# Joining 32x32 triangular inverses: four products beside each other, one transpose moved, and new due places, in a fused delta-rule attention and two feed-forward layers

## The chip, the cores and the metric

The kernel runs on one core of one Trainium2 chip (8 cores on the chip, 7 of them unused). The metric is the device time of one execution in microseconds (us). Before the change it is 960.64 us, the median of 3 runs (959.18 to 965.52 us).

## The reference, cut to what matters

Three layers in fp32: a delta-rule attention over 768 tokens (4 batches, 8 heads, head size 48), whose output of 3072 x 384 goes through a feed-forward layer with a squared ReLU (384 to 2048 to 384) and one with a maximum of three products (384 to 768 to 384).

```python
k_n = k / (np.linalg.norm(k, axis=-1, keepdims=True) + 1e-06)
for t in range(S):
    kt, vt, bt = (k_n[:, :, t], v[:, :, t], beta[:, :, t, None])
    y[:, :, t] = np.einsum('bhd,bhde->bhe', q[:, :, t], state)
    v_old = np.einsum('bhde,bhd->bhe', state, kt)
    state = state + bt[:, :, :, None] * np.einsum('bhd,bhe->bhde', kt, vt - v_old)
...
h = x @ w_in
r = np.maximum(h, 0.0)
out = (r * r) @ w_out
...
h = np.maximum(np.maximum(x @ w1, x @ w2), x @ w3)
out = h @ w_out2
```

## The kernel before, in words

**Stages.** The 768 tokens of each sequence are cut into six stages t of 128 tokens, and each stage into two chunks c of 64. A stage of attention is `gram(t)` (line 516: products of keys with keys into G, of queries with keys into W), `solve(t)` (line 602: the inverse of a triangular 64x64 matrix for each of 32 units, 16 for each chunk), `values(t)` and `chain(t)` (line 742: the state is carried through both chunks; the stages of it are Removed, Updates, State and `outputs`). `rows` (line 826) then sends the chunk's output from Y to xr with ten small transfers, `split` (line 861) splits xr into a high part xh and a low part xl, and `moe1(t)` (line 908) runs the first feed-forward layer for that stage: 16 slices f of w_in, each three matmuls of xh and xl with wih and wil for each of three rows of 128, then gh and gl with the slice of w_out, in fp32r. Where t is 0 the weights are prepared on the way (`load_w`, line 873: two passes on ScalarE, seven on VectorE for each of 32 pieces). For t = 0 the first 8 slices are done for the two chunks separately. The second feed-forward layer comes last, from about 540 us on. fp32 matmuls (attention) show as two instructions each in the trace, fp32r matmuls (the layers) as one.

**The inverse.** T is the inverse of each unit's triangular matrix of 64, in blocks of 32. Partitions hold four blocks of 32: two (0 to 31 and 32 to 63) for one head of a pair, two (64 to 95 and 96 to 127) for the other. A VectorE loop over 31 columns inverts all 32x32 diagonal blocks, two instructions a column (tmp, then T). T is transposed into Tn. The off-diagonal block is then made from two products with the block of K K^T that joins the halves: `solve` multiplies the joining block (in G, upper partitions, columns 32 to 63) with Tn into M1 (lines 697 to 711), and M1 with the transposed T in G into the result (lines 724 to 739). Both loops go over c, then n, then p0 in (0, 64); each matmul is 32x32, and the two of one n are on different partitions. ScalarE brings the sets of 64 matmuls from PSUM to M1 (four instructions of 32x512) and to G with a factor -1 (four of 32x512). Between the sets VectorE transposes T into columns 32 to 63 of G, ScalarE copies them to columns 0 to 31 on partitions 0 and 64, and POOL clears the lower left blocks. M1 is the memory of L.

```python
pl.vector.transpose(out=Tn.rearrange("p u k -> p k u"), in_=T.rearrange("p i k -> p k i"))
...
pl.vector.transpose(out=G[:, :, 32:64].rearrange("p u i -> p i u"), in_=T)
```

**What sets the order.** No engine's program is written by hand. Every call on `pl` is recorded (class `_Engine`, line 279; the call itself is made at line 324, which is therefore the line of all rows) with a cost and a due place `pl.at`, in units of one matmul group, 96 to a stage (TICKS). `Planner.issue` (line 253) plays the list forward from the due places, goes back from the end to get new due places, does so eight times, and issues the best order. Constants (line 375) set the due places: BOOST pulls an eviction ahead, DEC the weight pieces, CL the chain, GL the next `gram` and `solve`, SPL the reloads of w_out, LATE the second chunk in stage 0. MIX, FULL, STAY, BURST and URGENT (line 61) say when the planner goes from small fp32 matmuls to large fp32r ones and back. `together(beside=True)` makes several matmuls one step that is counted as lying beside each other; `gram` and `chain` use it, `solve` does not. The queues: all transfers are issued from SP. TensorE writes to eight PSUM banks: 0 to 2 for the results of `moe1`, 3 for its hidden part, 4 and 5 for `gram` and `solve`, 6 and 7 for `chain`; in stage 0 other rings are used, `first_ring` for the first chunk's chain (banks 2, 3, 0; line 840).

Of the kernel before, what the change touches and what calls it, by code (L numbers as in the profile page):

```python
# [52 lines left out]
class Planner:  # L53
# [6 lines left out]
    MIX, FULL, STAY, BURST, URGENT = 3816, 7024, 12.67, 1.78, 3.70  # L60
    INTO, BACK = 0.09, 0.2
    HOLD = {"vector": 0.06}
    LAG = {"tensor": 0.2, "vector": 0.13, "scalar": 0.15, "gpsimd": 0.08, "sync": 0.0}

    def __init__(self, nc):
        self.nc, self.at, self.ops, self.seen, self.joint, self.beside = nc, 0.0, [], {}, None, False
        self.free, self.first, self.end, self.before_all = {}, 0, {}, False
# [11 lines left out]
    def add(self, engine, call, cost, outs, ins, flow, late):  # L79
        if self.joint is None or self.joint == len(self.ops):  # L80
            self.ops.append([engine, [], 0.0, set(), self.at, any(a.dtype == F32R for a in ins), 0.0, 0.0, self.before_all])
# [32 lines left out]
    def forward(self, at):  # L114
# [20 lines left out]
        while todo:  # L135
# [14 lines left out]
            while r and r[0][0] <= t + self.HOLD.get(e, 0.0):  # L150
                when, n = heappop(r)
                heappush(q, (at[n], n))
                start[n] = when
# [24 lines left out]
            if e == "tensor":  # L178
# [4 lines left out]
                late = ops[n][7]  # L183
                if ticks.get(tick - 1, 0.0) < 3060:
                    cost *= 2
                    late *= 2
# [7 lines left out]
            if e == "sync":  # L194
                free[e] = t + 0.6
                free["dma"] = max(t + 1.3, free.get("dma", 0.0)) + cost
                end[n] = free["dma"] + 1.0
            else:
                free[e] = end[n] = t + cost
                if e == "tensor":  # L200
                    end[n] += late
# [77 lines left out]
class _Engine:  # L279
# [3 lines left out]
    def __getattr__(self, what):  # L283
        fn = getattr(getattr(self.plan.nc, self.name), what)

        def record(*args, **kw):
# [5 lines left out]
            cols = out.free_size()  # L292
# [13 lines left out]
            elif self.name == "vector":  # L306
                fast = what in ("tensor_scalar", "tensor_copy") and space != PSUM
                cost = (cols / (2 if fast else 1) + 64) / 960
                if what == "transpose":
                    cost = (cols * 1.8 + 64) / 960  # L310
                elif what == "reciprocal":
                    cost = (cols * 6 + 64) / 960
            elif self.name == "scalar":
# [7 lines left out]
            flow = late = 0.0  # L321
# [8 lines left out]
def kernel(  # L330
# [44 lines left out]
    GL, CL, G1, DEC, BOOST, SPL, CUT, HALF, G2, LATE, EARLY, BLOCKS, FIRST = 27, 51, -1, 97, 147, 41, 6, 8, -135, 155, 0, 3, 2  # L375
# [69 lines left out]
    Lx = one(apool, [P, 2, 528], F32, "L")  # L445
    Tx = one(apool, [P, 2, 528], F32, "T")
    L, T = (x.rearrange("p b n -> p (b n)")[:, 0:1024].rearrange("p (i k) -> p i k", i=32) for x in (Lx, Tx))
    Ld, Td = (x[:, :, 0:512].rearrange("p b (i k) -> p b i k", i=16)[:, :, :, 0:16] for x in (Lx, Tx))
    low = one(apool, [P, 2], F32, "low")
# [66 lines left out]
    def gram(t, at):  # L516

        pl.at = at
# [17 lines left out]
        def products(units, keys, queries):  # L536
# [65 lines left out]
    def solve(t, at):  # L602

        pl.at = at
# [26 lines left out]
        small = t < EARLY  # L631
        if small:
            for j in range(15):
                n, m = 15 - j, j + 1
                parts = (slice(0, 1), slice(1, 2)) if t == 0 else (slice(0, 2),)
                tv = [
                    tmp[:, 128 * x.start:128 * x.start + (x.stop - x.start) * n * m].rearrange(
                        "p (b n m) -> p b n m", n=n, m=m)
                    for x in parts
                ]  # L640
                for v, x in zip(tv, parts):
                    shape = [P, x.stop - x.start, n, m]
                    pl.vector.tensor_tensor(
                        v,
                        Ld[:, x, j + 1:16, j:j + 1].to_broadcast(shape),
                        Td[:, x, j:j + 1, 0:m].to_broadcast(shape),
                        op=ALU.mult,
                    )
                for v, x in zip(tv, parts):
                    pl.vector.tensor_tensor(  # L650
                        Td[:, x, j + 1:16, 0:m], Td[:, x, j + 1:16, 0:m], v, op=sub
                    )
                if j % 2:
                    adv(3)
        for j in range(0 if small else 31):
# [16 lines left out]
        if small:  # L672

            for c in range(2):
                px = a_ring().rearrange("p (u k) -> p u k", k=32)
                for u in range(NP):
                    for p0 in range(0, P, 32):
                        pl.tensor.matmul(
                            px[p0:p0 + 32, u], G[p0:p0 + 32, NP * c + u, 0:32],
                            Tn[p0:p0 + 32, NP * c + u], start=True, stop=True,  # L680
                        )
                pl.scalar.activation(M1[:, NP * c:NP * c + NP], px, AF.Copy)
            pl.vector.transpose(out=G[:, :, 0:32].rearrange("p u i -> p i u"), in_=T)
            for x in range(2):
                pz = a_ring().rearrange("p (u k) -> p u k", u=NU)
                for u in range(NU):
                    for p0 in range(0, P, 32):
                        p = slice(p0, p0 + 32)
                        left, right = (M1[p, u], G[p, u, 16:32]) if x else (G[p, u, 0:32], M1[p, u, 0:16])
                        pl.tensor.matmul(pz[p, u], left, right, start=True, stop=True)  # L690
                old = G[:, :, 16:32] if x else Tn[:, :, 0:16]
                pl.vector.scalar_tensor_tensor(
                    old, pz, low[:, x:x + 1], old, op0=ALU.mult, op1=ALU.add
                )
            adv(2)
        M1c, Gc = (x.rearrange("p (n c) k -> p c n k", c=2) for x in (M1, G))
        for c in range(2):
# [11 lines left out]
            for p0 in (32, 96):  # L709
                pl.scalar.activation(M1c[p0:p0 + 32, c], pm[p0:p0 + 32], AF.Copy)  # L710
            adv(1)
        pl.at -= LATE * (t == 0)
        if small:
            for p0 in (32, 96):
                pl.scalar.activation(G[p0:p0 + 32, :, 32:64], G[p0:p0 + 32, :, 0:32], AF.Copy)
                pl.gpsimd.memset(G[p0:p0 + 32, :, 0:32], 0.0)
        else:
            for p0 in (32, 96):
                pl.gpsimd.memset(G[p0:p0 + 32, :, 0:32], 0.0)
            pl.vector.transpose(out=G[:, :, 32:64].rearrange("p u i -> p i u"), in_=T)  # L720
            for p0 in (0, 64):
                pl.scalar.activation(G[p0:p0 + 32, :, 0:32], G[p0:p0 + 32, :, 32:64], AF.Copy)
        adv(2)
        for c in range(2):
            pl.at += LATE * c * (t == 0)
            pm = a_ring().rearrange("p (n x) -> p n x", n=NP)
            for n in range(NP):
                u = 2 * n + c
                for p0 in (0, 64):
                    pl.tensor.matmul(  # L730
                        pm[p0:p0 + 32, n, :],
                        M1[p0 + 32:p0 + 64, u, :],
                        G[p0 + 32:p0 + 64, u, 32:64],
                        start=True, stop=True,
                    )
            for p0 in (0, 64):
                pl.scalar.activation(
                    Gc[p0:p0 + 32, c, :, 32:64], pm[p0:p0 + 32], AF.Copy, scale=-1.0
                )
            adv(1)  # L740

    def chain(t, at):
        pl.at = at
# [82 lines left out]
        def rows(c):  # L826
            xv = xr.rearrange("p r (b c x) -> p r b c x", b=B, c=2)
            Yv = Y.rearrange("p (b a) x -> p a b x", b=B)
            for h in range(H):
                f0, e0 = h * D, 0  # L830
                while e0 < D:
# [3 lines left out]
                    pl.sync.dma_start(  # L835
                        out=xv[o:o + n, r, :, c, :], in_=Yv[p0:p0 + n, h // 2]
                    )
                    e0 += n

        first_ring = Ring([banks[2], banks[3], banks[0]])  # L840
# [145 lines left out]
    with tc.manual_schedule():  # L986
        make_identity(nc, ident)
        nc.gpsimd.memset(mask, 1.0)
        for p0 in (0, 64):
# [4 lines left out]
        nc.vector.tensor_reduce(  # L994
            out=low[:, 0:1], in_=ident.rearrange("p (q x) -> p q x", x=32)[:, :, 16:32],
            axis=mybir.AxisListType.XY, op=ALU.add, negate=True,
        )
        nc.vector.tensor_scalar(low[:, 1:2], low[:, 0:1], -1.0, -1.0, op0=ALU.mult, op1=ALU.add)
# [152 lines left out]
```

## Time and profile before

| | us |
|---|---|
| median of 3 runs | 960.64 |
| lowest and highest | 959.18, 965.52 |
| profiled execution | 961.32 |
| its span, first to last instruction | 959.4 |
| TensorE busy in the span | 889.5 (93%) |
| VectorE busy | 595.4 (62%) |
| ScalarE busy | 444.9 (46%) |
| mean granted clock of TensorE | 0.957 |

The rows name engines PE (TensorE matmuls), PEld (its weight loads), DVE (VectorE), ACT (ScalarE), POOL (GpSimd) and SP (the issuing of transfers). A row gives what is written, then what is read; a note in square brackets is the idle time of the engine just before and what ended it. Matmuls overlap, so their durations are longer than the distance between starts.

### The profile page before, as it was taken

Reading aid. Unit: us, or ns where it says so; the run is one execution under the profiler, and the core shown is the slowest. Engines: PE = TensorE matmul, PEld = TensorE weight load, DVE = VectorE, ACT = ScalarE, POOL = GpSimd, SP = SyncE. Lnnn points to the kernel's source line nnn. Section 1 sums busy time; section 2 is a strip of 40 time slices with the busy share of each in tenths; the row PEclk is TensorE's granted clock in tenths of the full one; section 3 lists DMA queues with packets and bytes.
Section 4 is the critical chain, followed back from the end, with each engine's and each line's share of the span. In section 5 each row is a group of like instructions: output and inputs, shape, how many; then the busy total and the mean of one; then the engine's idle time right before and its main releaser. Section 6 shows DMA issues by size and latency. Waiting matters only on the chain.

```text
span 959.4 us, 22394 instructions
## 1 busy us (share of the span) xinstructions
PE 889.5 (93%) x9388; PEld 745.0 (78%) x9388; DVE 595.4 (62%) x1258; ACT 444.9 (46%) x817; POOL 23.7 (2%) x33
## 2 busy tenths in 40 slices
PE   5446798999989998999999999999999999999998
PEld 4336698776877787877877788888898989898987
DVE  5999997899848966875963389893323232322221
ACT  6355367684365564475455567663222212121111
POOL 2001000010000000000000000000000000000000
PEclk9655799999999999999999999999999999999999
DMA  9754475677734745534522567661020100000000
GB/s 167 157 128 116 84 217 161 155 171 184 188 75 93 178 102 97 142 101 95 123 68 75 175 189 229 191 196 68 1 67 1 67 1 26 8 25 9 25 9 33
DMA packets 186276, 100.65 MB, mean 105 GB/s; under 512 B 150080, under 2 KB 166208, under 8 KB 186176
## 3 DMA queue, kind: packets, MB, share of 16 engines
q1 hardware_dynamic: 186176, 99.22, 40.1%
q8 instruction: 74, 1.21, 0.5%
q14 instruction: 26, 0.21, 0.1%
HBM read 79.53 MB, written 14.94 MB: 98 GB/s over the span
## 4 chain that ended last, share of the span: by engine, by line
PE 76%; DVE 13%; SPq 4%; DMA 3%; ACT 2%; issue 2%; DVEq 0%; ACTq 0%
PE ps L324 76%; SPq L324 4%; DVE xs L324 2%; DVE tmp L324 2%; DVE T L324 2%; DVE W L324 1%; DVE t L324 1%; DMA xr<-Y 1%; DMA qt<-in_q_dram 1%; ACT G L324 1%; DVE wo L324 1%; DVE gl L324 1%; DVE L L324 0%; DVE Tn L324 0%; DVE G L324 0%
## 5 line engine op out<-in xcount | busy, mean ns | idle before, releaser
L324 PE MATMUL ps<-gh,wo 128*128 128x512 f32 (+1 forms) x624 | 159.4, 385 | 3.3 <-ACT gh L324 1.7
L324 DVE TENSOR_TENSOR r<-r,ps 128x512 f32<-128x512 f32 x72 | 49.5, 688 | 178.7 <-PE ps L324 176.6
L324 ACT ACTIVATE r<-ps 128x512 f32<-128x512 f32 (+1 forms) x140 | 80.3, 573 | 157.0 <-PE ps L324 148.8
L324 PEld LDWEIGHTS ps<-gh,wo 128*128 128x128 f32 x624 | 112.2, 191 | 28.3 <-ACT gh L324 1.9
L324 PE MATMUL ps<-xh,wih 128*128 128x512 f32 (+1 forms) x312 | 123.4, 395 | 1.7 <-ACT r L324 1.7
L324 PE MATMUL ps<-xh,wil 128*128 128x512 f32 (+1 forms) x312 | 119.3, 382 | 0.3 <-DVE wil L324 0.3
L324 PE MATMUL ps<-xl,wih 128*128 128x512 f32 (+1 forms) x312 | 119.4, 383 | 0.0
L324 DVE TENSOR_TENSOR gl<-r,gh 128x512 fp32r<-128x512 f32 (+1 forms) x104 | 67.0, 645 | 40.6 <-ACT gh L324 37.3
L324 PE MATMUL ps<-gl,wo 128*128 128x512 f32 (+1 forms) x312 | 85.4, 382 | 0.0
L324 PEld LDWEIGHTS ps<-xh,wih 128*128 128x128 f32 x312 | 59.8, 192 | 15.5 <-ACT r L324 2.9
L324 PEld LDWEIGHTS ps<-xl,wih 128*128 128x128 f32 x312 | 59.9, 192 | 12.2
L324 PEld LDWEIGHTS ps<-xh,wil 128*128 128x128 f32 x312 | 60.1, 193 | 11.3 <-DVE wil L324 0.7
L324 ACT ACTIVATE gh<-r 128x512 fp32r<-128x512 f32 (+1 forms) x104 | 62.0, 596 | 10.9 <-PE ps L324 8.5
L324 PEld LDWEIGHTS ps<-gl,wo 128*128 128x128 f32 x312 | 56.4, 190 | 12.0
L324 DVE TENSOR_TENSOR tmp<-L,T 128x31 f32<-128x31 f32 (+15 forms) x186 | 62.9, 338 | 3.8
L324 DVE TENSOR_TENSOR T<-T,tmp 128x31 f32<-128x31 f32 (+15 forms) x186 | 62.9, 338 | 3.4
L324 ACT ACTIVATE r<-r 128x512 f32<-128x512 f32 (+1 forms) x104 | 62.1, 597 | 2.5
L324 PE MATMUL ps<-W 64*64 64x64 f32 x1536 | 44.8, 244 | 12.4 <-ACT W L324 11.3
L324 ACT ACTIVATE G<-ps 32x256 f32<-32x256 f32 (+2 forms) x96 | 46.4, 483 | 16.5 <-PE ps L324 14.7
L324 PEld LDWEIGHTS ps<-W 64*64 64x64 f32 x1536 | 37.7, 154 | 20.0 <-ACT W L324 14.0
L324 DVE TENSOR_SCALAR xs<-xs 128x384 f32<-128x384 f32 (+1 forms) x112 | 42.3, 380 | 16.4 <-ACT xs L324 15.5
L324 ACT ACTIVATE m0h<-r 128x512 fp32r<-128x512 f32 x18 | 11.4, 632 | 67.2 <-DVE r L324 67.2
(147 smaller groups left out, 1671.2 us busy)
## 6 DMA issues: line engine op xcount, KB each, us to landing
wo<-wod SPq DMA_DIRECT2D x88, 384.0 KB, 3.2
raw<-in_moe_w_out_dram SPq DMA_DIRECT2D x22, 384.0 KB, 3.6
raw<-in_moe_w_dram SPq DMA_DIRECT2D x18, 384.0 KB, 3.8
raw<-in_moe_w_in_dram SPq DMA_DIRECT2D x16, 384.0 KB, 4.1
wod<-wo SPq DMA_DIRECT2D x16, 384.0 KB, 3.2
vn<-in_v_dram SPq DMA_DIRECT2D x24, 192.0 KB, 4.5
kn<-in_k_dram SPq DMA_DIRECT2D x24, 192.0 KB, 4.9
out_dram<-ob SPq DMA_DIRECT2D x24, 192.0 KB, 1.9
```

The lines of the kernel that those rows point to most:

```text
L324: self.plan.add(self.name, lambda: fn(*args, **kw), cost, [out], ins, flow, late)
```

## The change

- In `solve`, the two products join the halves from the left in the even chunk (joining block times Tn, then the other half's inverse) and from the right in the odd one (the inverse in the upper partitions first, then Tn of the lower). A group of four matmuls, one step for the planner, lies on four blocks of partitions and four of results. The number of matmuls is the same, 64 a set.
- T is transposed straight into columns 0 to 31 of G, right behind the transpose into Tn and ahead of the first set; copies on partitions 32 and 96 bring it to columns 32 to 63, and the clearing on POOL follows the second set. One copy of 128x512 to M1 takes the place of four of 32x512.
- `gram` writes the lower joining block of the odd units as well, two more ScalarE copies for each call of `products` with odd units.
- In `rows`, five of the ten transfers of stage 0's first chunk are issued from ScalarE. `first_ring` has six places on four banks.
- The planner: MIX, BURST and HOLD change, the later ready time of large matmuls' results in the model is dropped, and nearly all due places change, with one offset for each stage of `gram`, `solve` and `chain`. EARLY was 0 and HURRY is 0: what hangs on them is not run.

```diff
-    MIX, FULL, STAY, BURST, URGENT = 3816, 7024, 12.67, 1.78, 3.70
-    INTO, BACK = 0.09, 0.2
-    HOLD = {"vector": 0.06}
+    MIX, FULL, STAY, BURST, URGENT = 3719.33, 7024.00, 12.67, 2.43, 3.70
+    INTO, BACK, RUSH = 0.09, 0.2, 0.52
+    HOLD = {"vector": 0.071}
...
-    GL, CL, G1, DEC, BOOST, SPL, CUT, HALF, G2, LATE, EARLY, BLOCKS, FIRST = 27, 51, -1, 97, 147, 41, 6, 8, -135, 155, 0, 3, 2
+    GL, CL, G1, DEC, BOOST, SPL, CUT, HALF, G2, LATE, BLOCKS, FIRST, HURRY = 27, 46, -1, 97, 164, 47, 6, 8, -133, 228, 3, 2, 0
+    GRAM = (0, -8, 0, 23, 17, 0)
+    SOLVE = (0, 0, 0, 80, 12, -33)
+    CHAIN = (-9, -8, 0, 11, -5, -19)
...
                     pl.scalar.activation(Gu[p, :, 0:32], pk[p, :, 32:64], AF.Copy)
+                    odd = slice(1, n, 2) if units.step is None else slice(0, n * (units.start % 2))
+                    if odd.stop:
+                        pl.scalar.activation(Gu[p, odd, 32:64], pk[p, odd, 0:32], AF.Copy)
...
-        for c in range(2):
-            pl.at += LATE * c * (t == 0)
-            pm = a_ring().rearrange("p (n x) -> p n x", n=NP)
-            for n in range(NP):
-                u = 2 * n + c
+        pl.vector.transpose(out=G[:, :, 0:32].rearrange("p u i -> p i u"), in_=T)
+
+
+        pm = a_ring().rearrange("p (n x) -> p n x", n=NP)
+        for n in range(NP):
+            with pl.together(beside=True):
                 for p0 in (0, 64):
+                    lo, hi = slice(p0, p0 + 32), slice(p0 + 32, p0 + 64)
+                    pl.tensor.matmul(pm[hi, n], G[lo, 2 * n, 32:64], Tn[lo, 2 * n], start=True, stop=True)
                     pl.tensor.matmul(
-                        pm[p0 + 32:p0 + 64, n, :],
-                        G[p0:p0 + 32, u, 32:64],
-                        Tn[p0:p0 + 32, u, :],
+                        pm[lo, n], G[hi, 2 * n + 1, 32:64], G[hi, 2 * n + 1, 0:32],
                         start=True, stop=True,
                     )
...
+        pl.scalar.activation(M1[:, 0:NP], pm, AF.Copy)
+        adv(1)
+        pa, pb = (a_ring().rearrange("p (n x) -> p n x", n=NP) for c in range(2))
+        for n in range(NP):
+            with pl.together(beside=True):
                 for p0 in (0, 64):
...
+                    lo, hi = slice(p0, p0 + 32), slice(p0 + 32, p0 + 64)
+                    pl.tensor.matmul(pa[lo, n], M1[hi, n], G[hi, 2 * n, 0:32], start=True, stop=True)
+                    pl.tensor.matmul(pb[lo, n], Tn[lo, 2 * n + 1], M1[lo, n], start=True, stop=True)
+        Gc = G.rearrange("p (n c) k -> p c n k", c=2)
+        for p0 in (0, 64):
+            for c, px in enumerate((pa, pb)):
+                p = slice(p0, p0 + 32)
+                pl.scalar.activation(Gc[p, c, :, 32:64], px[p], AF.Copy, scale=-1.0)
+        for p0 in (32, 96):
+            p = slice(p0, p0 + 32)
+            pl.scalar.activation(G[p, :, 32:64], G[p, :, 0:32], AF.Copy)
+            pl.gpsimd.memset(G[p, :, 0:32], 0.0)
...
-                    pl.sync.dma_start(
-                        out=xv[o:o + n, r, :, c, :], in_=Yv[p0:p0 + n, h // 2]
-                    )
+                    queue = pl.scalar if t + c == 0 and h % 2 else pl.sync
+                    queue.dma_start(out=xv[o:o + n, r, :, c, :], in_=Yv[p0:p0 + n, h // 2])
...
-        first_ring = Ring([banks[2], banks[3], banks[0]])
+        first_ring = Ring([banks[x] for x in (2, 3, 0, 7, 2, 3)])
```

## Rows read from the trace of the kernel before

**Rows 1.** The page: engines, slices of the span and a DMA queue (packets, MB, share).

```profile
PE 889.5 (93%) x9388; PEld 745.0 (78%) x9388; DVE 595.4 (62%) x1258; ACT 444.9 (46%) x817; POOL 23.7 (2%) x33
...
PE   5446798999989998999999999999999999999998
...
DVE  5999997899848966875963389893323232322221
...
PEclk9655799999999999999999999999999999999999
...
q8 instruction: 74, 1.21, 0.5%
```

**Rows 2.** Five stretches: busy us (instructions) of each engine, granted clock, DMA share, GB/s.

```profile
101.00:144.00 43.00, 40.03 (x547) 37.20 (x544) 41.19 (x108) 25.13 (x60) 0.00 (x0) 0.85 0.61 163
144.00:192.00 48.00, 43.12 (x927) 38.27 (x926) 37.40 (x79) 34.98 (x72) 1.27 (x2) 0.96 0.60 158
192.00:226.00 34.00, 31.08 (x217) 23.38 (x216) 32.77 (x82) 23.60 (x45) 4.06 (x6) 1.00 0.78 183
226.00:502.00 276.00, 268.35 (x4191) 217.18 (x4191) 206.26 (x420) 148.17 (x259) 8.62 (x9) 0.99 0.51 118
502.00:960.00 458.00, 453.25 (x2419) 383.61 (x2419) 189.53 (x344) 163.37 (x289) 0.00 (x0) 1.00 0.23 73
```

**Rows 3.** Timeline of PE: the a joining set of stage 1 and one of stage 2.

```profile
145.06 1.83 PE L324 MATMUL ps<-G,L 32*32 32x32 f32 x102
149.19 0.62 PE L324 MATMUL ps<-G,L 32*32 32x32 f32 x26 [2.31 <-issue]
...
265.82 2.21 PE L324 MATMUL ps<-Tn,G 32*32 32x32 f32 x128
267.96 0.50 PE L324 MATMUL ps<-xh,wih 128*128 128x512 f32 x1
```

**Rows 4.** Timeline of PE: a set of `gram`, four beside each other.

```profile
196.61 1.16 PE L324 MATMUL ps<-W 64*64 64x64 f32 x64
197.70 0.73 PE L324 MATMUL ps<-gh,wo 128*128 128x512 f32 x2
```

**Rows 5.** Timeline of all engines, 74 to 88 us: the tail of `solve(0)`.

```profile
74.34 1.92 DVE L324 STREAM_TRANSPOSE Tn<-T 128x1024 f32<-128x1024 f32 x1
...
76.31 3.63 PE L324 MATMUL ps<-Tn,G 32*32 32x32 f32 x128 [7.05 <-DVE Tn L324]
...
80.10 1.93 DVE L324 STREAM_TRANSPOSE G<-T 128x1024 f32<-128x1024 f32 x1
...
82.18 3.62 PE L324 MATMUL ps<-G,L 32*32 32x32 f32 x128 [2.24 <-DVE G L324]
...
85.73 2.54 PE L324 MATMUL ps<-vn,G 64*64 64x48 f32 x38
...
87.94 0.98 POOL L324 MEMSET G<- 32x1024 f32 x1 [4.83 <-DVE L L324]
```

**Rows 6.** Groups of ACT by shape: count, busy us, mean ns, idle before.

```profile
L324 ACT ACTIVATE G<-ps 32x256 f32<-32x256 f32 x48 | 18.1, 376 | 1.0
...
L324 ACT ACTIVATE L<-ps 32x512 f32<-32x512 f32 x24 | 14.2, 591 | 6.6 <-PE ps L324 6.4
...
L324 ACT ACTIVATE G<-G 32x1024 f32<-32x1024 f32 x12 | 12.7, 1054 | 1.8 <-DVE G L324 1.6
```

**Rows 7.** Timelines of SP and ACT: the first row transfers of stage 0.

```profile
95.60 7.31 SPq L324 DMA_DIRECT2D xr<-Y  x10
...
98.95 0.42 ACT L324 ACTIVATE xh<-xr 128x256 fp32r<-128x256 f32 x1 [3.37 <-DMA xr<-Y]
```

**Rows 8.** PE's waits, 226 to 960 us (us, times, longest), and a DMA queue (packets, MB, share), 265 to 300 us.

```profile
PE ps L324 <- issue: 4.9, 6, 2.3
...
q8 instruction: 8, 0.13, 1.5%
```

**Rows 9.** Groups of DVE: the column loop of `solve`.

```profile
L324 DVE TENSOR_TENSOR tmp<-L,T 128x31 f32<-128x31 f32 (+15 forms) x186 | 62.9, 338 | 3.8
```

More of the change, by code (lines that the diff above doesn't have):

```diff
@@ L66, in __init__ @@
         self.nc, self.at, self.ops, self.seen, self.joint, self.beside = nc, 0.0, [], {}, None, False
-        self.free, self.first, self.end, self.before_all = {}, 0, {}, False
+        self.free, self.first, self.end, self.before_all, self.rush = {}, 0, {}, False, False
         self.flow, self.ticks, self.start = (deque(), False, False), {}, {}
@@ L80, in add @@
         if self.joint is None or self.joint == len(self.ops):
-            self.ops.append([engine, [], 0.0, set(), self.at, any(a.dtype == F32R for a in ins), 0.0, 0.0, self.before_all])
+            self.ops.append([engine, [], 0.0, set(), self.at, any(a.dtype == F32R for a in ins), 0.0, 0.0, self.before_all, self.rush])
         n = len(self.ops) - 1
@@ L149, in forward @@
             r = ready.get(e, [])
-            while r and r[0][0] <= t + self.HOLD.get(e, 0.0):
+            hold, later = self.HOLD.get(e, 0.0), []
+            while r and r[0][0] <= t + (self.RUSH if hold else 0.0):
                 when, n = heappop(r)
-                heappush(q, (at[n], n))
-                start[n] = when
+                if when <= t + hold or ops[n][9]:
+                    heappush(q, (at[n], n))
+                    start[n] = when
+                else:
+                    later.append((when, n))
+            for x in later:
+                heappush(r, x)
             n = q[0][1]
@@ L199, in forward @@
                 free[e] = end[n] = t + cost
-                if e == "tensor":
-                    end[n] += late
+                if e == "scalar":
+                    end[n] += ops[n][7]
             todo -= 1
@@ L291, in record @@
                 ins.append(out)
-            cols = out.free_size()
+            cols, late = out.free_size(), 0.0
             space = ins[0].space if ins else None
@@ L312, in record @@
                     cost = (cols * 6 + 64) / 960
+            elif what == "dma_start" and self.name == "scalar":
+                cost, late = 0.65, 2.0
             elif self.name == "scalar":
@@ L320, in record @@
                 cost = words / row * 0.00142 if row < 128 else words * 4 / (220e3 if row < 512 else 290e3)
-            flow = late = 0.0
+            flow = 0.0
             if self.name == "tensor":
@@ L444 @@
     bl = one(apool, [P, NS, 32], F32, "bl")
[L445 to L449, printed above, removed]
+    L = one(apool, [P, 32, 32], F32, "L")
+    T = one(apool, [P, 32, 32], F32, "T")
     st = one(apool, [P, 5, 32], F32, "st")
@@ L516, in gram @@
     def gram(t, at):
-        pl.at = at
+        pl.at = at + GRAM[t]
         W, G = W2[t % 2], GG[t % 2]
@@ L630, in solve @@
         adv(2)
[L631 to L647, printed above, removed]
-                    )
[L649 to L655, printed above, removed]
+        for j in range(31):
             n, m = 31 - j, j + 1
@@ L671, in solve @@
         adv(2)
-        if small:
-            for c in range(2):
[L675 to L695, printed above, removed]
@@ L713, in solve @@
[L713 to L722, printed above, removed]
@@ L723, in solve @@
[L723 to L728, printed above, removed]
-                for p0 in (0, 64):
[L730 to L740, printed above, removed]
+        pl.scalar.activation(M1[:, 0:NP], pm, AF.Copy)
@@ L742, in chain @@
+        for p0 in (0, 64):
[6 more added lines that the diff above has]
+            pl.gpsimd.memset(G[p, :, 0:32], 0.0)
+        adv(1)
+        pl.rush = False
     def chain(t, at):
-        pl.at = at
+        pl.at = at + CHAIN[t]
@@ L993 @@
             )
[L994 to L998, printed above, removed]
         pl.at = -3 * TICKS
```

11 lines of the change are left out of this document (1 added, 10 removed).

## The prediction

> **What bounds the kernel now.** I read the page first, then stretches. The page [rows 1] gives TensorE 889.5 us busy, 93% of the span, and in its 40 slices the matmul digits are 9 and the clock digit is 9 from about the tenth slice on; before it both are low, and VectorE stands at 8 or 9 instead. So there are two limits: a head in which VectorE prepares weights and the first two stages of attention, and then a long stretch in which the matmul engine has no room.
>
> The table by stretch [rows 2] puts the border near 226 us. From 226 to 502 us TensorE is busy 268.35 of 276 us, from 502 to 960 us 453.25 of 458 us. There a microsecond of matmul time removed is nearly a microsecond of the span. From 101 to 144 us it is busy 40.03 of 43 us at a mean granted clock of 0.85, and from 144 to 192 us 43.12 of 48 us; VectorE is busy 41.19 of 43 us, 37.40 of 48 us and, just before the border, 32.77 of 34 us. In the head, then, a gain on TensorE counts only in part.
>
> The profiled execution took 961.32 us (span 959.4 us and 1.9 us around it), 0.7 us above the median of 960.64 us. The sum below is made against 961.32 us; the last step takes the 0.7 us off. A measurement of this kernel can tell about 1%, which is 9.6 us.
>
> **The joining products, stages 2 to 5.** Each call of `solve` issues two sets of 64 fp32 matmuls, which the trace shows as two times 128 instructions of 32x32. The timeline has the first set of stage 2 [rows 3], which stands for the eight of stages 2 to 5, all alike: 128 instructions from 265.82 us, and the next large matmul 2.14 us later, at 267.96 us. Only two of them run beside each other (partitions 0 to 31 and 64 to 95), and 2.14 us over 128 is 16.7 ns an instruction. The change issues the same 128 instructions a set (16 values of n with four matmuls, instead of 32 pairs), but on four places of the array that share neither rows nor columns.
>
> The trace before has no group of four at 32x32, so this is bounded from both sides. Nearest row: the products of `gram` are groups of four on 64x64, and 64 instructions at 196.61 us take until 197.70 us, the next start, which is 17.0 ns each [rows 4]. They move 64 columns for 64 weights, twice the 32 columns of the joins, and cost the same each: four beside each other at 64 columns go as fast as two at 32. Halving the columns with four still beside each other gives half, 8.5 ns, or 1.1 us a set. The bad end is no gain, 2.14 us. The good end is 0.9 us, if the 64x64 groups were held up by something other than columns. I take 1.1 us, so 1.0 us is saved on each set. Eight sets in stages 2 to 5: **-8.0 us**.
>
> The Trainium skill ("TensorE: Matmul & The Clock Gate", Part 1, on the floors of small matmuls) says that start-to-start never falls below about 25 ns however few columns there are. By that rule 128 instructions need 3.2 us and the term would be nothing. The 16.7 ns above already lies under that floor, so the row and the rule differ, and I go by the row; what such a floor for tiles would do here is a rival below.
>
> **Stage 1.** Its second set begins at 145.06 us and goes on, after a standstill, at 149.19 us [rows 3]. The stretch has TensorE busy nine tenths of the time [rows 2], so two sets of 1.0 us count 0.9 each: **-1.8 us** (0 to -4, the latter if the 2.31 us standstill inside the second set goes as well).
>
> **Stage 0, the tail of `solve`.** Before [rows 5]: VectorE starts the transpose into Tn at 74.34 us, TensorE runs set one from 76.31 us for 3.63 us (the clock digit is 5 there, which is its lower level, 1.2 GHz [rows 1]), VectorE transposes T into G only at 80.10 us (it must wait until set one has read G), set two runs from 82.18 us, and the first Updates matmul is at 85.73 us, 11.4 us after the start. After: both transposes back to back (1.92 + 1.93 us) until 78.2 us; set one at half clock 1.8 us, 80.0 us; one copy of 128x512 instead of four of 32x512, 0.6 us and about 0.6 us of handing over, 81.2 us; set two, 83.0 us. Then two scalings of 0.59 us each [rows 6], and, new at this place, the memset of G's lower left on POOL, which must now wait for set two since set two reads it; before, it was off the path. Two memsets took 0.98 us each, the one at 87.94 us is shown. That ends near 85.2 us: **-0.5 us** (+2 to -2). The copies of G to G (1.05 us each) now run beside set two. What could uncover them is ScalarE, which is shared with weight work.
>
> **ScalarE.** `gram` gains copies of the lower block for odd chunks: eight calls of 32x128 in each of the stages 0 to 2, four of 32x256 (0.376 us [rows 6]) in the others. `solve` loses three of its four 0.59 us copies. That is about +1 us a stage early and about nothing later, on an engine that is busy 25.13 of 43 and 148.17 of 276 us [rows 2]. I cost it at nothing; in stage 0, where the copies stand in front of the transpose of L, it is up to +3 us.
>
> **The row transfers of stage 0.** SP issues the ten small transfers of the first chunk one after the other in 7.31 us [rows 7], and the first of ScalarE's conversions behind them waited 3.37 us. Five of them now go to ScalarE's queue, so about 5 x 0.7 = 3.6 us of issuing goes from SP and about as much comes to ScalarE, which was idle there. But the matmuls that follow are soon held by weights from VectorE. I count under half: **-1.5 us** (0 to -3.6). The larger ring of banks in `chain(0)` takes away waits of results for banks; there VectorE orders the work, and I cost it at nothing.
>
> **Instruction delivery.** TensorE's waits after 226 us [rows 8] have 4.9 us on "issue", six times, the longest 2.3 us: it waited for nothing that the profile shows. In 265 to 300 us the instruction queue q8 made 8 fetches of together 0.13 MB, one per 4.4 us, in a stretch full of small matmuls. Per fetch that is some 16 KB, and 128 matmuls with their 128 weight loads, a set, would be about one fetch if an instruction has 64 bytes (an estimate: the page's 1.21 MB over 74 fetches, divided by 18,776 TensorE instructions, is 64 bytes [rows 1]). Faster sets use up a block in 1.1 us. Where bursts touch, some of the gain returns as standstill: **+1.5 us** (0 to +8). The Trainium skill ("Runtime: NRT & Kernel Launch", Instruction fetch mechanics) holds that fetching the next page is mostly hidden. By it this term would be nothing and the sum 1.5 us lower; the standstills of 2.3 us in a straight-line kernel speak against it.
>
> **The new due places.** Nearly all numbers that set the planner's order change (BOOST 147 to 164, CL 51 to 46, one offset per stage for `gram`, `solve` and `chain`, the thresholds of mixing). They remove no instruction. What they can win is idle time: VectorE stands idle 48 - 37.40 = 10.6 us from 144 to 192 us [rows 2], while just after it the weights are late and VectorE alone decides. Attention of stages 0 and 1 moves about 8 ticks earlier, which fills such holes. What they can lose is shown as a rival. Between -10.6 and +21 us I take a quarter of the hole: **-2.5 us**.
>
> Sum: -8.0 - 1.8 - 0.5 - 1.5 + 1.5 - 2.5 = -12.8 us; 961.3 - 12.8 = 948.5 us, and in terms of the median 948 us.
>
> **The rivals.**
> - *Delivery takes it all back.* If each faster set ends in a standstill, the terms of stages 1 to 5 vanish: 961.3 - 0.5 - 1.5 - 2.5 = 956.8 us, or 956 us as a median, within 1%. For it: the standstills [rows 8] lie where small matmuls are dense. Against it: most sets stand between large matmuls [rows 3], which give the fetch time.
> - *The four don't run beside each other*, as a floor per instruction would have it. The sum is the same, 956 us, but the sets would keep their 2.2 us. Against it: the groups of four on 64x64.
> - *The head gives back its whole hole.* All 10.6 us instead of 2.5 us: 948.5 - 8.1 = 940.4 us, 940 us as a median. For it: VectorE is the limit in the head and the hole is in front of its busiest part. Against it: ScalarE has 34.98 us of work in those 48 us [rows 2], and what VectorE waits for there need not come sooner.
> - *Slower: weights arrive late.* If stage 1's attention moves ahead of weight preparation on VectorE, its column loop, 62 instructions of 0.338 us (31 of each of two kinds a stage; the 186 of one kind are shown, the other's mean is the same [rows 9]), 21.0 us, stands in front of weights that stage 0's matmuls wait for. TensorE then idles up to 21 us: 961.3 - 10.3 + 21.0 = 972 us (10.3 is the sum without the last term). It decides once stage 0 has used up the weights in hand. For it: `gram(1)` and `chain(1)` move 8 ticks earlier and the weights' place DEC stays. Against it: the planner weighs what is late.
>
> **How the numbers follow.** Forecast 0.50 (942 to 955 us), head wins more 0.18, delivery 0.15, no concurrency 0.06, slower 0.11. Faster by over 1% means under 951.0 us: nearly nine tenths of the forecast and the second case, 0.62. Within 1%: the rest of the forecast, delivery and no concurrency, 0.27. Slower: 0.11. The range leaves out a tenth at each end: 934 to 964 us.
>
> **What would show it.** Right: the 32x32 sets last about 1.1 us in stages 2 to 5 with four starts close together; TensorE's matmul time between the border and the end falls by some 8 us with no more than 2 us of new "issue" waits; the first conversion of xr starts about 3 us sooner after the outputs. Wrong: sets still of 2 us; "issue" waits grown to 10 us; VectorE still holed in the head; or large matmuls waiting for wil or wo around 100 to 225 us, which would show the slower case.

## The result, and the profile after

The changed kernel takes 949.94 us (median of 4 runs, 947.98 to 951.66) beside 960.49 us before: ratio 0.988, 95% interval 0.9838 to 0.9922. Forecast were 948 us, between 934 and 964 us. The profiled execution took 948.75 us (span 946.6 us) against 961.32 us, 12.6 us less; the sum said 12.8 us. Two runs of the experiments, of 1450 and 2152 us, in a far slower state, are left out of the times and ratios below.

The page after, with the rows that answer to [rows 1]: engines, slices of PE, DVE and clock, and the queue of instructions.

```profile
PE 879.0 (93%) x9388; PEld 733.6 (77%) x9388; DVE 588.9 (62%) x1256; ACT 443.7 (47%) x835; POOL 23.3 (2%) x33
...
PE   5536789999999989999999999999999999999998
...
DVE  4999998899758957955953499893323232323221
...
PEclk9555799999999999999999999999999999999999
...
q8 instruction: 73, 1.20, 0.5%
```

TensorE has the same 9388 matmuls. The same stretches as in [rows 2] (busy us and count of each engine, clock, DMA share, GB/s):

```profile
101.00:144.00 43.00, 39.45 (x459) 36.13 (x459) 42.48 (x115) 23.59 (x58) 0.00 (x0) 0.88 0.55 153
144.00:192.00 48.00, 45.79 (x1125) 39.60 (x1124) 42.44 (x89) 42.00 (x92) 5.20 (x7) 1.00 0.76 195
192.00:226.00 34.00, 33.81 (x198) 26.34 (x197) 33.88 (x91) 19.55 (x35) 0.00 (x0) 1.00 0.65 177
```

VectorE's hole from 144 to 192 us has shrunk from 10.6 to 5.6 us, and from 192 to 226 us TensorE is now full. Since both kernels issue the same large matmuls, the records can be laid beside each other by their number. Where both have issued 350 x 512 columns of large matmuls and the same 2368 small ones, before stands at 239.49 us and after at 232.09 us: the head gave 7.4 us. When attention is over the lead is 12.6 us and stays there: stages 2 to 5 took 5.2 us less.

One of the eight sets of stages 2 to 5, a first set, first matmul and next large one, as in [rows 3], in the timeline of PE:

```profile
333.52 0.21 PE L330 MATMUL ps<-Tn,G 32*32 32x32 f32 x1
333.52 0.21 PE L330 MATMUL ps<-G 32*32 32x32 f32 x1
333.53 0.21 PE L330 MATMUL ps<-Tn,G 32*32 32x32 f32 x1
...
334.61 0.19 PE L330 MATMUL ps<-G 32*32 32x32 f32 x1
334.73 0.73 PE L330 MATMUL ps<-gl,wo 128*128 128x512 f32 x2
```

128 instructions take 1.21 us where they took 2.14 us: 0.93 us a set. All four first sets and one second set go like that. The three other second sets stand still once for 0.7 to 0.8 us between two starts and take 1.95 to 2.04 us; this one is of the same stage:

```profile
336.33 0.21 PE L330 MATMUL ps<-G,L 32*32 32x32 f32 x1
...
337.82 0.21 PE L330 MATMUL ps<-G,L 32*32 32x32 f32 x1 [0.61 <-issue]
...
338.36 0.50 PE L330 MATMUL ps<-xh,wih 128*128 128x512 f32 x1
```

These standstills are among PE's waits. The waits from 226 us on (us, times, longest), after first, then those of before that [rows 8] leaves out:

```profile
PE ps L330 <- issue: 9.0, 13, 1.6
PE ps L330 <- ACT US L330: 1.2, 2, 1.0
PE ps L330 <- ACT r L330: 0.4, 2, 0.2
```

```profile
PE ps L324 <- ACT Y L324: 2.2, 2, 1.9
PE ps L324 <- ACT US L324: 0.5, 2, 0.3
PE ps L324 <- DVE Tn L324: 0.4, 1, 0.4
PE ps L324 <- DVE wo L324: 0.2, 1, 0.2
```

"Issue" went from 4.9 to 9.0 us. Waits for other engines there fell from 3.3 us (ScalarE 2.7, VectorE 0.6) to 1.6 us. So 8 x 0.93 = 7.4 us won, 4.1 us given back at issue, 1.7 us won from other waits: 5.0 us, against the 5.2 us that the records show. That agreement is closer than the sum deserves, since a term is missing. Before has a granted clock of 0.95 from 265 to 300 us (half clock for 3.4 us, 1.5 us after the end of its standstill of 2.3 us), after has 1.00 there, and 0.05 x 35 us makes some 1.7 us more that were won:

```profile
265.00:300.00 35.00, 31.92 (x983) 26.53 (x982) 21.57 (x31) 21.36 (x41) 2.85 (x3) 0.95 0.39 77
```

With it the sum is 6.7 us; what took 1.5 us of that away is not shown.

### The profile page after: what moved, and what is told of

Read it like the earlier page. It is cut to its first block, busy times and chain, and to the rows that moved or that the text cites. A ratio compares the mean times of both kernels' runs of the same rounds, so it can differ in the third digit from the quotient of the medians.

```text
span 946.6 us, 22413 instructions
## 1 busy us (share of the span) xinstructions
PE 879.0 (93%) x9388; PEld 733.6 (77%) x9388; DVE 588.9 (62%) x1256; ACT 443.7 (47%) x835; POOL 23.3 (2%) x33
## 4 chain that ended last, share of the span: by engine, by line
PE 78%; DVE 14%; ACT 4%; issue 2%; DMA 1%; DVEq 0%; ACTq 0%
PE ps L330 78%; DVE xs L330 3%; DVE T L330 2%; DVE tmp L330 2%; DVE t L330 2%; ACT G L330 1%; DVE W L330 1%; DMA raw<-in_moe_w_in_dram 1%; DVE L L330 1%; ACT W L330 1%; ACT r L330 1%; DVE wil L330 1%; ACT US L330 1%; DVE gl L330 0%; DVE US L330 0%
## 5 line engine op out<-in xcount | busy, mean ns | idle before, releaser
L330 ACT ACTIVATE G<-ps 32x256 f32<-32x256 f32 (+3 forms) x132 | 55.4, 432 | 22.5 <-PE ps L330 20.4
L330 PE MATMUL ps<-W 64*64 64x64 f32 x1536 | 47.0, 249 | 12.3 <-ACT W L330 9.7
L330 PEld LDWEIGHTS ps<-W 64*64 64x64 f32 x1536 | 40.2, 159 | 19.2 <-ACT W L330 12.2
L330 DVE TENSOR_SCALAR xs<-xs 128x384 f32<-128x384 f32 x112 | 40.6, 362 | 16.4 <-ACT xs L330 15.6
L330 ACT ACTIVATE m0h<-r 128x512 fp32r<-128x512 f32 x18 | 11.4, 632 | 67.2 <-DVE r L330 67.2
```

The source lines that it names most:

```text
L330: self.plan.add(self.name, lambda: fn(*args, **kw), cost, [out], ins, flow, late)
```

## The experiments

**The two halves apart.** Two kernels. The first keeps the join and `gram`'s copies and has before's `Planner`, constants, SP queue and ring:

```diff
-    MIX, FULL, STAY, BURST, URGENT = 3719.33, 7024.00, 12.67, 2.43, 3.70
+    MIX, FULL, STAY, BURST, URGENT = 3816, 7024, 12.67, 1.78, 3.70
...
-    GRAM = (0, -8, 0, 23, 17, 0)
+    GRAM = (0,) * 6
...
-                    queue = pl.scalar if t + c == 0 and h % 2 else pl.sync
+                    queue = pl.sync
```

> The join alone: products four beside each other, direct transpose and gram's extra copies, with the planner constants, due places, row queue and ring of before. Theory (the sets carry the matmul-bound part, the places the head): sets of about 1.1 us, 8 x 1.06 = 8.5 us less in stages 2 to 5, some 3 us of it returned as issue waits, about 1 us from stages 0 and 1: 954 us (951 to 957). Rival (the new due places carry the gain): 958 to 961 us.

Measured: 954.3 us, 0.9939 (0.9924 to 0.9954). The second has the new planner, places, queue and ring with before's products, transpose and copies:

```diff
-                    pl.tensor.matmul(pm[hi, n], G[lo, 2 * n, 32:64], Tn[lo, 2 * n], start=True, stop=True)
...
+                    pl.tensor.matmul(
+                        pm[p0 + 32:p0 + 64, n, :], G[p0:p0 + 32, u, 32:64], Tn[p0:p0 + 32, u, :],
...
```

> Everything but the join: planner constants, due places, row queue and ring of after, with the two products, transpose and copies of before (LATE at its new 228). Theory: the sets stay at 2.1 us, the head is some 5 us shorter: 955 us (953 to 959), and the matmul time after the head is as before. Rival (places carry it all): 949 to 952 us. Second rival (the places only fit the join): 960 us or more.

Measured: 953.6 us, 0.9932 (0.9915 to 0.9949). Alone they give 6.4 and 7.0 us; together 10.5, not 13.4 us. The join alone even makes the head longer: at the same 350 x 512 columns it stands at 247.36 us, 7.9 us behind before, and wins everything later. Here is the stretch from 350 to 1400 x 512 columns, the same matmuls in all four kernels: before, the places alone, the join alone, after.

```profile
239.49:583.04 343.55, 335.53 (x4795) 271.07 (x4794) 237.89 (x488) 190.25 (x334) 8.62 (x9) 1.00 0.49 123
235.91:574.17 338.26, 333.45 (x4795) 269.73 (x4794) 228.26 (x463) 190.34 (x331) 8.58 (x9) 1.00 0.49 122
247.36:576.49 329.13, 326.00 (x4795) 262.43 (x4794) 226.60 (x459) 186.48 (x332) 10.46 (x11) 1.00 0.49 125
232.09:570.40 338.31, 327.84 (x4795) 263.18 (x4794) 234.71 (x481) 187.98 (x334) 10.45 (x11) 1.00 0.50 125
```

The places alone, with sets of 2.14 us, win as much there (5.3 us) as the whole change (5.2 us), and the join alone wins 14.4 us. TensorE's waits make the difference: in this stretch they are 7.9 us before, 4.7 us with the places, 3.1 us with the join and 10.5 us after. Sets (7.4 us where they are fast), waits and the clock of before (1.7 us) add up to 5.0 us for the places, 14.0 us for the join and 6.6 us for after. "Issue" alone is 2.4 us with the join, less than before, although its sets are as fast as those of after:

```profile
PE ps L324 <- issue: 2.4, 4, 1.2
```

**The join with the second queue, on the old places.**

```diff
-                    queue = pl.sync
+                    queue = pl.scalar if t + c == 0 and h % 2 else pl.sync
```

> The join alone (constants and due places of before) plus the row transfers on two queues. If the new queue moves the head by the place it gives the weights, the last weight piece comes earlier than the 232 us of the join alone and the time falls below 954 us by about as much: 948 us (944 to 953). If the due places do that, 954 us.

Measured: 950.6 us, 0.9913 (0.9884 to 0.9943). The last weight piece on VectorE starts at 220.34 us instead of 232.28 us. The new due places, with the larger ring of banks, add nothing that can be measured to this: 950.6 against 949.9 us, with overlapping intervals. This kernel and three below (transfers on SP in the same order, two places, without the column loop) ran in a round in which before took 959.0 us, 1.5 us less than in the round of after. Against that before, the join and the queue give 8.4 us where the whole change gives 10.5 us, so some 2 us for the due places are not excluded.

**The queue of the row transfers.** First with a new plan:

```diff
-                    queue = pl.scalar if t + c == 0 and h % 2 else pl.sync
+                    queue = pl.sync
```

> The kernel after with all ten row transfers of stage 0's first chunk on SP again (the planner makes a new order of it). Theory of the prediction: 1.5 us slower, 951.5 us (950 to 954). Rival (the first conversion of xr waits as long as before, only the third comes sooner, and weights decide there): 950 us, no difference.

Measured: 965.9 us, 1.0063 (1.0041 to 1.0084), slower than before. VectorE's timeline has the end of the weight pieces, and the stretch 216 to 240 us shows TensorE short of work (the same stretch of after behind it):

```profile
237.28 0.55 DVE L330 TENSOR_TENSOR wo<-xs,wo 128x384 fp32r<-128x384 f32 x1
...
216.00:240.00 24.00, 15.56 (x84) 11.36 (x84) 22.37 (x59) 9.46 (x17) 0.00 (x0) 0.86 0.55 157
```

```profile
217.01 1.02 DVE L330 TENSOR_TENSOR wo<-xs,wo 128x384 fp32r<-128x384 f32 x2
...
216.00:240.00 24.00, 23.59 (x126) 18.17 (x125) 20.97 (x41) 9.35 (x17) 0.00 (x0) 1.00 0.82 202
```

Here weights come late, but not in the way of the rival: the column loop of stage 1 runs from 93.9 to 134.8 us, after has it from 92.9 to 134.3 us. It is stage 2's loop, from 197.0 us on with six pieces still to come, that stands between them: it has 17.0 us of VectorE before the last piece starts, against 6.2 us in after and 4.0 us before. TensorE's longest standstill shows how that reaches it. It ends with ScalarE's r, which comes behind a weight pass that waited for VectorE:

```profile
228.25 0.52 ACT L330 ACTIVATE wo<-xs 128x384 fp32r<-128x384 f32 x1 [3.49 <-DVE xs L330]
228.91 0.60 ACT L330 ACTIVATE r<-ps 128x512 f32<-128x512 f32 x1
...
229.56 0.80 PE L330 MATMUL ps<-xh,wih 128*128 128x512 f32 x1 [5.63 <-ACT r L330]
```

To part the queue from the plan, the same order with the five calls made on SP at the same place:

```diff
-            self.plan.add(self.name, lambda: fn(*args, **kw), cost, [out], ins, flow, late)
+            call = self.plan.nc.sync.dma_start if what == "dma_start" else fn
+            self.plan.add(self.name, lambda: call(*args, **kw), cost, [out], ins, flow, late)
```

> The kernel after with the very order of after on every engine; only the five row transfers of stage 0 that ScalarE issued are issued by SP at the same place of the order. Theory (the transfers themselves are worth little, the 16 us of the re-planned kernel came from weights that VectorE prepares late): 950 to 953 us, the last weight piece at 217 to 221 us. Rival (the second queue itself is worth the 16 us): 960 us or more.

Measured: 953.7 us (951.5 to 958.8), 0.9957 (0.9934 to 0.998). The queue is worth some 4 us by the medians (5 us against the before of each round), not 16. The third conversion of xr comes at 106.3 us instead of 101.4 us, and VectorE stands still in front of its xl; its waits for ScalarE's xh from 95 to 145 us:

```profile
DVE xl L331 <- ACT xh L331: 2.7, 1, 2.7
```

In after VectorE has no such wait in that stretch, and before has none in front of its first three xl either. The last weight piece starts at 220.8 us instead of 217.5 us.

**What makes the sets faster.** Same order, but of two neighbouring steps the four matmuls on the same two places are issued first, then the four on the other two:

```diff
+                for k in (0, 1):
+                    for call in ops[held][1][k::2] + ops[n][1][k::2]:
+                        call()
```

> The kernel after with the same order on every engine, except that of two neighbouring steps of a set the four matmuls on the same two places of the array are issued first, then the other four, so that only two lie beside each other. Theory: sets take 2.1 us again, 8 x 1.06 = 8.5 us more in stages 2 to 5 less some 4 us of issue waits that go, 1 to 2 us more in stages 0 and 1: 955.5 us (953 to 959), issue waits in the matmul-bound part back from 9.0 to about 5 us. Rival (waits have nothing to do with the pace of the sets): 960 us with 9 us of issue waits. Second rival (four don't run beside each other): 950 us, no change.

Measured: 950.3 us, 0.9891 (0.9869 to 0.9914): no change, a miss. The timeline of PE:

```profile
336.44 0.22 PE L347 MATMUL ps<-Tn,G 32*32 32x32 f32 x2
336.46 0.22 PE L347 MATMUL ps<-G 32*32 32x32 f32 x2
336.49 0.20 PE L347 MATMUL ps<-Tn,G 32*32 32x32 f32 x2
336.52 0.19 PE L347 MATMUL ps<-G 32*32 32x32 f32 x1
...
337.76 0.50 PE L347 MATMUL ps<-gl,wo 128*128 128x512 f32 x1
```

The program has four of one kind (eight instructions), then four of the other; the starts in the records alternate by pairs, and the set takes 1.32 us. By these records TensorE finds the free places by itself. The second rival (four don't run beside each other) fits the time but not this row. What decides must then be how many places a set uses, so the next kernel has as many instructions on two places:

```diff
-            for call in ops[n][1]:
+            for call in [ops[n][1][x] for x in (0, 2, 0, 2)] if n in self.joins else ops[n][1]:
```

> The kernel after with its order, each group of four matmuls made of the two of the even chunk, issued twice; the odd chunk's are left out (its off-diagonal blocks are not computed). As many instructions as after, but a whole set uses two places of the array instead of four. Theory (the number of places sets the pace, TensorE finds the free one by itself): sets take 2.1 us, 8 x 1.0 us more less 2 to 4 us of issue waits that go: 955 us (952 to 958). Rival (the pace comes from the number of matmuls alone): sets of 1.1 us and 950 us.

Measured: 953.7 us, 0.9945 (0.9918 to 0.9971). One set, and PE's waits from 226 us:

```profile
337.47 2.21 PE L331 MATMUL ps<-Tn,G 32*32 32x32 f32 x128
339.61 0.73 PE L331 MATMUL ps<-gl,wo 128*128 128x512 f32 x2
...
PE ps L331 <- issue: 3.9, 6, 1.1
```

2.14 us a set as before, and 5.1 us of issue waits gone: 8 x 0.93 - 5.1 = 2.3 us (3.9 us with the issue waits of the repeat of after below, 7.4 us). Measured are 3.8 us by the medians and 4.1 us between the profiled executions, of which the records put 2.7 us into the head and 1.4 us behind it. The number of places sets the pace, and in this order of the program most of what it wins in stages 2 to 5 comes back as issue waits. The join alone shows that another order gives back nothing.

**Delivery of instructions.** That "issue" waits are waits for instructions can be read from the traces themselves. Of all records of TensorE (matmuls, weight loads and the few others of its queue) in order of time, the one that ends an issue wait behind 226 us always has a number that leaves 193 or 194 when divided by 256: so it is for all 6 waits of before, 13 of after, 4 of the join alone and 15 of after doubled, and in every other kernel here whose trace can be used. The queue q8 fetches some 16 KB for each 256 of them, and each of these waits ends 2.2 to 3.0 us after the start of a fetch, 1.2 to 1.8 us after its last packet. They stand at the borders of blocks. How often a border falls into a dense stretch would then be a matter of the order, which fits the 2.4 us of the join alone.

What the waits cost was tried with three kernels: the order of after with each group of four issued twice, then before's with each matmul of the sets twice, then after's with every second group left out:

```diff
-            for call in ops[n][1]:
+            for call in ops[n][1] * (1 + (n in self.joins)):
...
-            for call in ops[n][1]:
+            for call in [] if n in self.joins and n % 2 else ops[n][1]:
```

> The kernel after with the same order, each group of four issued twice (same operands, same result): 1536 more matmul instructions and as many weight loads. Theory (delivery of instructions at some 3.5 us per 256 sets the pace of dense stretches): beyond the array's own 1.1 us per set each set waits 1 to 2.5 us more: 972 us (966 to 985), issue waits over 18 us in the matmul-bound part. Rival (array time alone): 8 x 1.08 + 2 to 4 us = 961 us, issue waits as they are, 9 us.

> The kernel before, its order unchanged, each matmul of the sets issued twice (same operands, same result): the same 1536 instructions and weight loads more as in the doubling of after. Theory (delivery): what they cost is set by their number, not by the array, so the time comes near that of the doubled after, 1000 us (994 to 1008), and the gain of the change is nearly gone at that load. Rival (array time, two beside each other): 12 x 2.0 = 24 us, 985 us (980 to 988).

> The kernel after with the same order, but every second group of four of each set is left out (half of the off-diagonal blocks are not computed): 32 of 64 matmuls a set, 128 fewer TensorE instructions a set, half a fetch. Theory (dense stretches run at some 4 us per 256 instructions, as the doubling showed: 52 us for 12 x 256): up to 2 us a set, less in the head, where VectorE decides: 934 us (928 to 941), issue waits under 5 us in the matmul-bound part. Rival (only the doubled load met the limit; at the load of after the array's time counts): 12 x 0.54 = 6.5 us at most, 944 us or more, issue waits near 9 us.

Measured: 1002.3, 1016.1 and 942.3 us (1.0449, 1.0592 and 0.9816). The queue and PE's waits from 226 us, doubled after first, half after second:

```profile
q8 instruction: 86, 1.41, 0.6%
...
PE ps L331 <- issue: 24.1, 15, 3.0
```

```profile
q8 instruction: 67, 1.10, 0.5%
...
PE ps L331 <- issue: 4.6, 7, 1.2
```

Doubling adds 3072 instructions, 12 blocks of 256 (the page counts 86 fetches in both kernels, 74 in before, 73 in after and 74 in its repeat below), and costs 52.4 us on top of after and 55.6 us on top of before. The waits grow as the theory had it (24.1 us, over 18 us expected), but both times are beyond their ranges, and neither theory nor rival holds for them: by the theory the two doubled kernels should nearly meet, and they lie 13.7 us apart, more than the change gives; by the rival only the array's time should count, 11 to 13 and 24 us. Three costs come together. The stretch of equal work, after doubled and before doubled:

```profile
252.03:622.19 370.16, 344.41 (x5819) 276.83 (x5818) 234.61 (x481) 188.32 (x334) 10.44 (x11) 0.98 0.46 115
```

```profile
251.51:638.19 386.68, 368.65 (x5820) 300.05 (x5818) 238.34 (x488) 190.29 (x334) 8.62 (x9) 0.95 0.43 110
...
PE ps L325 <- issue: 16.4, 14, 2.0
```

After doubled is 31.9 us longer there: some 9.5 us of array time (8 x 1.19), 15.1 us more of issue waits, and a granted clock of 0.98 instead of 1.00, about 7 us. Before doubled is 43.1 us longer: 17 us of array time (8 x 2.14), 11.5 us of issue waits, and a clock of 0.95, about 19 us (the terms overlap). So the array's time counts as well, and 52.4 us cannot be shared out as a price per fetch.

Leaving out half saves 7.7 us. In time that is nearer to the rival's 6.5 us at most than to the 16 us of the theory; in waits it is as the theory has it, since issue falls from 9.0 to 4.6 us and the rival wanted 9 us.

**How much VectorE still holds the head.** Stage 1's column loop left out, the order kept:

```diff
+            if t == 1:
+                pl.ops[-1][1], pl.ops[-2][1] = [], []
```

> The kernel after with its order, without the 62 instructions of stage 1's column loop on VectorE (21.0 us; the inverse of stage 1 is left at its diagonal). Theory (VectorE's weight pieces set the end of the head): the last piece comes 10 to 20 us earlier and TensorE's idle time between 101 and 226 us, some 10 us, mostly goes: 941 us (936 to 946). Rival (the head waits for attention's own chain): 948 us or more.

Measured: 944.9 us, 0.9854 (0.9815 to 0.9893), from three runs, without a trace that could be used. That is 5.0 us less than after, or 3.5 us less when each is taken against the before of its round, for 21.0 us of VectorE's work. The theory's range holds at its weak end by the first figure; by the second the time lies between theory and rival. The traces speak more plainly for it: in all 13 kernels with a usable one, the mark of 350 x 512 columns comes 13.7 to 17.2 us after the start of VectorE's last weight piece, while that piece itself moves from 217 to 237 us.

**A repeat.** BOOST at 160:

> The kernel after with BOOST at 160 instead of 164, a small shift of one due place, to see how far neighbouring orders lie apart. If the due places are worth what one number says, 950 us within 1 us. If orders scatter with every small change, as the difference between the join alone and the places alone suggests, 953 us within 4 us, with other issue waits.

Measured: 949.3 us, 0.989 (0.9867 to 0.9913). The order came out the same on every engine, so this is a second measurement of after, 0.7 us from the first, and says nothing of neighbouring orders. How far those can lie is seen above: 965.9 us when one queue was taken back and the planner made a new order. The repeat's issue waits behind 226 us are 7.4 us where after has 9.0 us: these vary by over 1 us between executions of one order.

## Why the prediction was right

The total was right within 2 us, and so were its two parts: the head 6.3 us forecast (all terms but the first and the delivery), 7.4 us found; stages 2 to 5 6.5 us forecast, 5.2 us found. The mechanism of the first term, four places instead of two, is shown. That the parts came out so close is in part luck: inside, several terms were mis-sized or had another cause, a stretch at half clock in before was left out, and the places alone win as much in stages 2 to 5 as the whole change.

- *The sets in stages 2 to 5, -8.0 us.* 0.93 us each, 7.4 us, without the standstills. The bound by the 64x64 groups held (1.21 us against 1.1 us). Its reason, four neighbours in the program, was only half of it: the places of the whole set count, not the grouping.
- *Stage 1, -1.8 us.* Its two sets, each from its first matmul to the next of another kind, took 2.66 and 4.69 us and take 2.36 and 1.97 us, 3.0 us less, most of it the standstill in the second one (2.5 us between two starts, now 0.7 us). How much of that reaches the end of the head is not shown.
- *Instruction delivery, +1.5 us.* Too small: issue waits rose by 4.1 us (2.5 us in the repeat), more than the 2 us that the prediction allowed as a sign of being right. It put them down to the pace of the sets; the join alone has that pace and 2.4 us of such waits, so the order decides as well. The rival, that all comes back, did not happen. The Trainium skill ("Runtime: NRT & Kernel Launch", Instruction fetch mechanics) calls the crossing of a block mostly hidden. Among the large matmuls after 530 us the trace of after agrees, with no issue wait at all; in the stretches of small ones it doesn't, with 13 waits of together 9.0 us.
- *The tail of stage 0, -0.5 us.* Not shown as a gain. The timelines of after:

```profile
75.23 1.97 DVE L330 STREAM_TRANSPOSE Tn<-T 128x1024 f32<-128x1024 f32 x1
...
84.44 1.94 POOL L330 MEMSET G<- 32x1024 f32 x2 [4.38 <-PE ps L330]
...
85.43 0.44 PE L330 MATMUL ps<-vn,G 64*64 64x48 f32 x2 [1.08 <-POOL G L330]
86.43 3.22 PE L330 MATMUL ps<-vn,G 64*64 64x48 f32 x54 [0.56 <-POOL G L330]
```

Against [rows 5] the transpose starts 0.9 us later, and the memset on POOL, put on the path by the change as the prediction said, holds the Updates twice, 1.6 us in all. The first matmul came at 85.43 us (85.2 us forecast), the second memset let the rest go only at 86.43 us; before, all went from 85.73 us on. From the start of the transpose that is 10.2 and 11.2 us, against 11.4 us before: the tail is a little shorter, and the later start takes it away.
- *The row transfers, -1.5 us.* Too small, some 4 us, and for another reason. The first conversion of xr is not sooner, as forecast by 3 us, but later (99.88 against 98.95 us [rows 7]); the third is sooner by 3.1 us, and with it VectorE doesn't stand still in front of the weights, as it does when after's order is kept with all ten on SP. Before, in its own order, has no such standstill, so the 4 us hold for after's order.
- *The new due places, -2.5 us.* Nothing clear of the noise on top of join and queue (950.6 against 949.9 us, up to some 2 us by rounds). Without the join they and the queue give 7.0 us.
- *Late weights.* The rival was right in that late weights decide the head: they make the kernel with the transfers back on SP 16 us slower, 972 us forecast and 965.9 us found. The loop that comes between is stage 2's, not stage 1's as the rival had it. After has the last piece at 217 us, before at 225 us; that is the head's gain.

What stays open: which due place moved which weight piece, and how the planner's order puts the borders of instruction blocks into dense stretches. That the halves alone add up to 2.9 us more than both together is what is left of two larger differences. In the profiled executions they win 14.4 + 5.3 us behind the mark, where both together win 5.2 us, and -7.9 + 3.6 us ahead of it, where both together win 7.4 us.

## What to carry to other kernels

Where two small matmuls leave places of the array free, spread a whole set over more places; the order inside the set need not be written out. Count instructions too: a dense stretch of small matmuls that runs faster can meet the delivery of its instructions, so look at the "issue" waits before and after, and at where in the stream they stand. Lay two kernels beside each other by equal work before you call a sum right: here it showed a clock term and an order term that the totals hid. And where one engine prepares weights in order, the end of its last piece tells more of the head than any busy share.

## What the runs showed that was not expected

- TensorE starts fp32 32x32 matmuls out of program order when their place is free: 1.32 us a set with four matmuls of a kind in a row, 1.21 us with alternating ones, 2.14 us on two places. The Trainium skill ("TensorE: Matmul & The Clock Gate", Part 3, the mechanism) has matmuls start in strict order of the program; the starts in the kernel with pairs differ from that.
- Every "issue" wait behind 226 us, 4 to 15 of them in the kernels named, stands at the same place of each 256 instructions of TensorE and ends 1.2 to 1.8 us after a fetch of q8 has landed.
- 12 more blocks of such instructions cost 52.4 us and 55.6 us, as array time, issue waits and a lower granted clock together.
- A planner's new order after one queue was changed moved the time by 16 us, more than the whole change.
